# A two-branch transformer block on one core: the order of the first stage rewritten, with 25 identity products ahead of it

## The chip, the core and the metric

The kernel runs on one core of a Trainium2 chip. The core has five engines that run their own instruction streams and meet at semaphores: TensorE (PE in the profile; its weight loads are shown apart as PEld) for matrix products, VectorE (DVE), ScalarE (ACT), GpSimd (POOL), and SyncE (SP), which here issues all DMAs. Products land in PSUM (eight banks); the other operands lie in SBUF; inputs, outputs and larger intermediate results lie in HBM. The metric is the device time of one execution in microseconds, and a kernel's time is the median of its runs.

## What is computed

`x` has 2048 rows of 640 numbers, all in float32. One attention branch with 32 heads of 20 numbers and one MLP branch with shifted columns run on the same layer-normed rows, and both are added to `x`:

```
xn  = layernorm(x)
q, k, v = split(xn @ wqkv)                       # 32 heads of 20
A   = (softmax(q k^T / sqrt(20)) v) @ wo
h   = gelu(layernorm(xn) @ w1)
x1  = xn + shifted(h) @ w2                       # four column groups, rows shifted by +1, -1, +2, -2
B   = x1 + gelu(layernorm(x1) @ w3) @ w4         # w3: 640x1536
out = x + A + B
```

## The kernel before

**Products.** Most products are made in single-pass float32 (fp32r) from operands split in two: a high part (a rounded copy) and a low part (the operand less its high part). A product of two such operands is three: high with high, high with low, low with high. `parts` (L707) lists them for the five 128-row pieces of the contraction, the three of one piece behind each other. `twins` (L711) makes two such sums at once, each on half of the array's rows; it does so in two turns of 15 steps, and between the turns stands a fence (`fence`, L329): a one-element memset on GpSimd (`scratch`) that waits for the first turn's last product and for which the second turn waits. All products, transposes aside, are recorded at L346, and all operations of the other engines at L316.

**Order.** The kernel first lists all operations with their data dependences, a cost and a key (a due time). `schedule` (L389) then plays them through in a small model and emits the program in the order that comes out, engine by engine; each engine keeps that order on the chip. Operations marked `port=True` on VectorE and GpSimd are not planned to overlap, and an operation can be moved to another engine if `alt` says so. For TensorE a string of 7058 letters, `ORDER` (L95), says which kind comes next: `m` a pair of products for the row maxima of the scores, `s` a pair of products for the scores, `p` the products with v, and `d` anything else. Among the `d`s the smallest key that is ready goes first.

**The first stage** (L775 to L911) loads x in 16 tiles of 128 rows (`load_x`, tiles `xb`), the first half of wv in five pieces (`wvr`, of which four borrow the buffers `vst`), and the first 128 columns of wk and wq (`load_w0`). On SP's queue stand two x tiles, wv, two x tiles, wk, wq, and then the other x tiles. `norm_tiles` (L836) takes x tiles in groups: tiles 0 and 1, tiles 2 and 3, then four at a time. Per tile VectorE takes the statistics (two `bn_stats`, one `bn_aggr`). Per group `rsqrt` (L657) makes the reciprocal root: one small VectorE operation, a power on GpSimd (`ry_a`), and three small VectorE operations (`rt_a`, `rt_a`, `lnk`); a fourth makes the bias `lnk[:, 1]`. The tiles are then normalised, the even ones on VectorE and the odd ones on ScalarE, and transposed by TensorE (`tp`); ScalarE rounds the high part of `xT` out of PSUM, and VectorE subtracts the low part. ScalarE rounds and GpSimd subtracts the weights: `split_wv` (L825) for wv, whose subtractions wait for the first group's power, and `load_w0` (L790) for wk and wq (`w0s`), whose subtractions wait for the second group's.

With four tiles transposed, a pair of `twins` makes 512 columns of k and q for the first heads (`ps0`, L880), and two small products (`pk`) put them in the layout of the attention loop. This is done four times. v's first half (`v_half`, L946, tiles `psv`) uses `xT` and wv and can run from the first transposed pair on. The maxima products of the first block then follow among these, and the attention loop starts when that block's 64 pairs of maxima are reduced on VectorE (`mx`).

**Behind it** the attention loop runs over 32 blocks of 32 units, and the `d` products of all other matrices are spread between its products: k, q, v of the other heads, w1 (`w1_phase`, L959, which reads the row factors `r2b` by a DMA for every 512 columns), w2 with the second layernorm (`x1_pair`, `z_pair`), w3 (with `pre3`, gelu and a store), w4 (`w4_phase`, L1147), and last wo (`wo_phase`, L1192).

## Time and profile before

| | |
|---|---|
| median of 3 runs | 1882.86 us (1882.71 to 1885.95) |
| the profiled execution | 1883.12 us |
| its span in the profile | 1881.3 us |
| mean granted TensorE clock | 0.998 |
| DMA moved | 262.00 MB, 139 GB/s over the span |

The profile is one execution. Its page gives each engine's busy time, the span in 40 slices, the chain of work that ended last, and the costliest groups of instructions. A group reads: line, engine, operation, what is written from what, shape, count. A number in square brackets in the timeline is the engine's idle time just before the instruction and what ended it. "Stretches" are windows of the span, in microseconds from its start, with the busy time of each engine. The granted clock is TensorE's, 1.00 being full speed. The ends of matrix products are modelled, so that a busy TensorE is not always one at its peak.

### The profile page before, as it was taken

What the parts mean: (1) busy time and instruction counts of PE and PEld (TensorE: products, weight loads), DVE (VectorE), ACT (ScalarE), POOL (GpSimd) and SP (SyncE); (2) the same over time, 40 slices, a digit from 0 to 9 for tenths busy, and PEclk for the clock granted to TensorE, in tenths of its full rate; (3) what the DMA queues carried; (4) which work ended last, traced back from release to release, by engine and by line L of the source; (5) the groups of instructions that cost most, each with busy time, mean ns of one, the idle gap of its engine ahead of it and who ended that gap; (6) DMA issues with size and microseconds to landing.
All of it is one profiled execution on the core that took longest, in us unless ns stands there. A gap on an engine that the chain in (4) does not pass through costs nothing.

```text
span 1881.3 us, 44229 instructions
## 1 busy us (share of the span) xinstructions
PE 1857.6 (99%) x17185; PEld 1272.1 (68%) x17185; DVE 1568.9 (83%) x2766; ACT 1333.1 (71%) x2456; POOL 383.7 (20%) x586
## 2 busy tenths in 40 slices
PE   6999999999999999999999999999999999999998
PEld 5876666565666657676665757665877777675777
DVE  8979888888889989988788988878887889788724
ACT  4267767877877786777887676778677776768761
POOL 4101111212112112212212311111222222212111
PEclk9999999999999999999999999999999999999999
DMA  4664554646454585655435672434523242343403
GB/s 166 175 169 142 151 120 149 186 147 180 128 156 141 160 230 160 200 155 160 132 126 189 196 223 93 125 101 132 138 72 95 77 115 84 81 132 112 146 13 113
DMA packets 232666, 262.00 MB, mean 139 GB/s; under 512 B 60776, under 2 KB 175928, under 8 KB 230656
## 3 DMA queue, kind: packets, MB, share of 16 engines
q1 hardware_dynamic: 232456, 259.17, 46.7%
q8 instruction: 135, 2.21, 0.5%
q14 instruction: 75, 0.61, 0.1%
HBM read 155.84 MB, written 103.25 MB: 138 GB/s over the span
## 4 chain that ended last, share of the span: by engine, by line
PE 94%; DVE 3%; DMA 2%; ACT 1%; POOL 0%; issue 0%; SPq 0%; DVEq 0%; POOLq 0%; ACTq 0%
PE ps L346 26%; PE pv L346 24%; PE pm L346 14%; PE s L346 14%; PE psv L346 4%; PE pso L346 3%; PE ps_k L346 3%; PE ps_q L346 3%; DVE mx L316 1%; PE psl L346 1%; DMA wd_wo<-ph_wo 0%; DMA wd_w<-ph_w 0%; DMA r2b<-r2d 0%; PE pmt L346 0%; PE c_w L346 0%
## 5 line engine op out<-in xcount | busy, mean ns | idle before, releaser
L316 DVE TENSOR_REDUCE mx<-pm 128x1 f32<-128x512 f32 x2048 | 1281.5, 682 | 195.9 <-PE pm L346 181.4
L316 ACT ACTIVATE p<-s 128x512 f32<-128x512 f32 x2048 | 1080.5, 612 | 282.9 <-PE s L346 237.7
L346 PE MATMUL pv<-p,v 128*32 128x512 f32 x4096 | 494.4, 598 | 0.2 <-DVE mx L316 0.2
L346 PE MATMUL pm<-kpack,zq 60*128 60x512 f32 x2048 | 446.3, 411 | 0.6 <-DVE mx L316 0.5
L346 PE MATMUL s<-zq,kpack 62*128 62x512 f32 x2048 | 443.5, 410 | 1.4 <-ACT p L316 0.8
L346 PE MATMUL ps<-xT,w_w 64*128 64x512 f32 x2040 | 321.5, 394 | 0.0
L346 PEld LDWEIGHTS s<-zq,kpack 62*128 62x128 f32 x2048 | 229.4, 185 | 122.7 <-ACT p L316 39.8
L346 PEld LDWEIGHTS pm<-kpack,zq 60*128 60x128 f32 x2048 | 230.9, 185 | 118.3 <-issue 31.7
L346 PEld LDWEIGHTS pv<-p,v 128*32 128x32 f32 x4096 | 109.2, 109 | 224.4 <-issue 195.2
L346 PEld LDWEIGHTS ps<-xT,w_w 64*128 64x128 f32 x2040 | 211.8, 186 | 34.6 <-issue 2.9
L316 POOL TENSOR_TENSOR ob<-ob,obq 128x512 f32<-128x512 f32 x96 | 123.7, 1289 | 391.5 <-ACT obq L316 292.3
L346 PE MATMUL ps<-xT 64*128 64x320 f32 x1632 | 166.3, 307 | 0.0
L346 PEld LDWEIGHTS ps<-xT 64*128 64x128 f32 x1632 | 145.2, 186 | 10.5 <-issue 1.7
L346 PE MATMUL ps<-xT,gT 64*128 64x320 f32 x1152 | 121.0, 307 | 0.0
L316 ACT COPY obq<-pv 128x512 f32<-128x512 f32 x75 | 44.1, 588 | 106.2 <-PE pv L346 105.9
L346 PEld LDWEIGHTS ps<-xT,gT 64*128 64x128 f32 x1152 | 107.7, 186 | 6.2 <-DVE mx L316 0.8
L334 POOL MEMSET scratch<- 1x1 f32 x134 | 11.9, 89 | 432.6 <-PE ps L346 220.0
L346 PE MATMUL psv<-wv,xT 64*128 64x320 f32 x960 | 92.4, 310 | 0.0
L346 PEld LDWEIGHTS psv<-wv,xT 64*128 64x128 f32 x960 | 82.5, 186 | 6.2 <-POOL scratch L334 1.0
L316 POOL TENSOR_TENSOR ph_w<-pr_w,ph_w 128x320 fp32r<-128x320 f32 (+2 forms) x54 | 40.6, 752 | 210.7 <-ACT ph_w L316 157.5
L346 PE MATMUL ps_q<-xT,w_q 64*128 64x512 f32 x480 | 77.4, 394 | 0.0
L346 PE MATMUL ps_k<-xT,w_k 64*128 64x512 f32 x480 | 75.1, 395 | 0.0
(172 smaller groups left out, 1355.0 us busy)
## 6 DMA issues: line engine op xcount, KB each, us to landing
zq<-qd SPq DMA_DIRECT2D x156, 80.0 KB
kpack<-kd SPq DMA_DIRECT2D x78, 160.0 KB
w_w<-wd_w SPq DMA_DIRECT2D x48, 256.0 KB
gd<-pre SPq DMA_DIRECT2D x8, 1536.0 KB
g<-gd SPq DMA_DIRECT2D x64, 192.0 KB
wd_w<-ph_w SPq DMA_DIRECT2D x34, 320.0 KB
xT<-wd_w SPq DMA_DIRECT2D x34, 320.0 KB
vd<-vst SPq DMA_DIRECT2D x32, 256.0 KB
```

The lines of the kernel that those rows point to most:

```text
L316: getattr(e, m)(val(out), *[val(x) for x in ins], **{k: val(v) for k, v in kw.items()})
L334: o.insts = [nc.gpsimd.memset(scratch.get(), 0.0)]
L346: o.insts = [nc.tensor.matmul(out.get(), lhsT.get(), rhs.get(), **kw) for out, lhsT, rhs, kw in products]
```

## The change

In the first stage:

- SP issues four x tiles, then wv, wk and wq, then the other x tiles.
- `norm_tiles` is cut in two, `norm_rows` (statistics, roots, normalising) and `turn_tiles` (transposes, high and low parts). The rows of tiles 0 to 3 are listed ahead of their transposes, in two groups as before. Statistics of tile 4 are planned behind the second group's bias, and the low parts of tiles 0 and 1 behind the start of the second root.
- The subtractions on GpSimd of all five wv pieces, wk and wq wait for the second group's bias.
- A group `warm` of 25 products of the identity with itself (float32, 128x128) is put on TensorE; it needs only the identity, and its result is not read.
- `phases` lists a sum's products so that all five pieces of one kind (high with high, and so on) stand together. The first k/q products and v take the products with a low weight last.
- VectorE's root operations are planned with `port=True`, and the memsets of `vst` without.

Farther on: `r2b` is read once in four DMAs instead of for each of 20 tiles; the ring of `x1` has 2 buffers instead of 3; the odd shifted tiles (`hs`), `pre3` and `r` get pools of their own, opened before the pool ahead of them is closed; in `w4_phase` the even tiles instead of the odd ones put `gT` in `xT`, and the first product of a tile waits for the buffer of `r`. `ORDER` has 7059 letters: one `d` more and as many `m`, `s` and `p` as before; most of its lines differ, by letters moved a few places, and the last 582 letters are the same.

```diff
+WARM = 25
+WVE = 0
...
-    "dddddddddddddddddd")
+    "ddddddddddddddddddd")
...
+    ps = ps_x.shared([P, 512], F32, "warm", "s")
+    pl.group("full", WARM * 320.0, [(ps[:, :P], ident, ident, dict(start=True, stop=True))] * WARM)
...
-    def rsqrt(pool, v, n, nm, out=None):
+    def rsqrt(pool, v, n, nm, out=None, port=True):
...
+    def phases(lhs, rhs, kts, ab):
+
+        return [(lhs(a, k), rhs(b, k)) for a, b in ab for k in kts]
...
-    load_x(2)
+    load_x(4)
...
-    load_x(2)
-    pl.key += 1
     load_w0(1, "k0")
     load_w0(0, "q0")
...
-            pl("pool", c_pool(320), "tensor_sub", vw0[1][:, 1, i, :], wvr[i], _f(vw0[1][:, 0, i, :]),
-               port=True).deps.append((after, 1))
+            wvs.append(pl("pool", c_pool(320), "tensor_sub", vw0[1][:, 1, i, :], wvr[i], _f(vw0[1][:, 0, i, :]), port=True))
...
-    def norm_tiles(ts):
+    def norm_rows(ts):
...
+        if ts[0] == 2:
+            pl.key -= 2
         for j, t in enumerate(ts):
             stats(lnp, xbs[t], mva[:, t, :], f"a{t}")
+            if t == 4:
+                for o in pl.ops[-3:-1]:
+                    o.deps.append((nbs[-1], 0))
...
         rsqrt(lnp, mva[:, tr, 1], n, g, lnk[:, 0, tr])
+        rvs.append(next(o for o in pl.ops[first:] if o.eng == "dve"))
+        nb = pl("dve", 140.0, "scalar_tensor_tensor", lnk[:, 1, tr], mva[:, tr, 0], -1.0, lnk[:, 0, tr],
+                op0=ALU.mult, op1=ALU.mult, port=True)
+        nbs.append(nb)
         if ts[0] == 0:
-            split_wv(pl.ops[-5])
-        if ts[0] == 2:
-            for o in w0s:
-                o.deps.append((pl.ops[-5], 1))
...
+            split_wv()
+        for o in {0: wvs[:WVE], 2: wvs[WVE:] + w0s}.get(ts[0], ()):
+            o.deps.append((nb, 1))
...
+    def turn_tiles(ts):
...
-            pl("dve", c_dve(m * n * P), "tensor_sub", l, v, _f(h))
+            o = pl("dve", c_dve(m * n * P), "tensor_sub", l, v, _f(h))
+            if ts[0] == 0:
+                o.deps.append((rvs[1], 0))
...
-            norm_tiles(range(4 * tb + g[0], 4 * tb + g[1]))
+        for g in gs:
+            norm_rows(g)
+        for g in gs:
+            turn_tiles(g)
...
-        twins(pss, [parts(lambda p, k: w0[e][:, p, k, :], lambda p, k: xT[:, p, k, sl], range(ND)) for e in (1, 0)], 512)
+        twins(pss, [phases(lambda p, k: w0[e][:, p, k, :], lambda p, k: xT[:, p, k, sl], range(ND),
+                           ((0, 0), (0, 1), (1, 0))) for e in (1, 0)], 512)
...
-        pl("pool", 500.0, "memset", v, 1.0, port=True)
+        pl("pool", 500.0, "memset", v, 1.0)
...
-            twins(pss, [parts(lambda p, k: xT[:, p, k, t * P:(t + 1) * P], lambda p, k: w[:, p, k, :], range(ND))
-                        for t in (t2, t2 + 1)], 320)
+            twins(pss, [phases(lambda p, k: xT[:, p, k, t * P:(t + 1) * P], lambda p, k: w[:, p, k, :], range(ND),
+                               ((0, 0), (1, 0), (0, 1))) for t in (t2, t2 + 1)], 320)
...
+        r2b = wp.tile([P, S], F32, name="r2b")
+        for tb in range(4):
+            dma(r2b[:, tb * 512:(tb + 1) * 512], r2row[:, tb * 512:(tb + 1) * 512].to_broadcast([P, 512]), 262144)
...
-                x1 = sp.tile([P, 2, D], F32, tag="x1", name=f"x1_{q}", bufs=3)
+                x1 = sp.tile([P, 2, D], F32, tag="x1", name=f"x1_{q}", bufs=2)
...
-                    ring.append(sp.tile([P, GB, S // 2], F32, tag="pre3", name=f"pre3_{half}_{f}", bufs=2))
+                    ring.append(rp.tile([P, GB, S // 2], F32, tag="pre3", name=f"pre3_{half}_{f}", bufs=2))
...
-            if t % 2:
+            if t % 2 == 0:
...
-            twins(pss, [parts(lambda p, k: gT[p][k], lambda p, k: w4v(k, n)[:, p, :], range(NF)) for n in range(2)], 320)
+            twins(pss, [parts(lambda p, k: gT[p][k], lambda p, k: w4v(k, n)[:, p, :], range(NF)) for n in range(2)], 320,
+                  room=r)
```

More of the change, by code (lines that the diff above doesn't have):

```diff
@@ L823, in tile_kernel, with split_wv @@
     load_x(XB - 4)
-    def split_wv(after):
+    def split_wv():
         k, pl.key = pl.key, -903.0
@@ L857, in norm_tiles @@
         pl.key += 4
+    def turn_tiles(ts):
+        n = len(ts)
         w = 512 // (P * n)
@@ L1045, in w23_phase @@
         xrp = pl.pool(name="xrp", bufs=2)
-        sp = None
         hs0 = hs_load(0)
         st1.close()
+        rp = None
         for half in range(2):
-            sp = pl.pool(name=f"s3p{half}", bufs=2, side="right")
+            sp = pl.pool(name=f"s3x{half}", bufs=2, side="right")
+            if rp:
+                rp.close()
+            hsp = pl.pool(name=f"s3h{half}", bufs=1, side="right")
             def x1_pair(q, hs):
-                x1 = sp.tile([P, 2, D], F32, tag="x1", name=f"x1_{q}", bufs=3)
+                x1 = sp.tile([P, 2, D], F32, tag="x1", name=f"x1_{q}", bufs=2)
                 mv = sp.tile([P, 2, 2], F32, tag="mv3", name=f"mv3_{q}")
@@ L1099, in w23_phase @@
             z_pair(4 * half + 3, prev)
+            hsp.close()
             sp.close()
@@ L1107, in w23_phase @@
                 gs = [load_g(gp, 0)]
+            rp = pl.pool(name=f"s3r{half}", bufs=2)
             sp = pl.pool(name=f"s3q{half}", bufs=2, side="right")
@@ L1145, in tile_kernel, with w4_phase @@
     W4_ALL = [(k, n) for k in range(NF) for n in range(2)]
-    def w4_phase(gp, gs):
+    def w4_phase(gp, gs, pre):
         fill["part"] = "w4"
+        rp = pl.pool(name="s4r", bufs=2, side="right")
+        pre.close()
         sp = pl.pool(name="s4p", bufs=1, side="right")
@@ L1178, in w4_phase @@
         sp.close()
+        rp.close()
         xtp.close()
```

152 lines of the change are left out of this document (77 added, 75 removed).

## The prediction

> **What bounds the kernel now.** I read the page first, then stretches of the span by engine, then the timeline of the first 33 us, then who waits for whom. From the page:
>
> ```profile
> span 1881.3 us, 44229 instructions
> PE 1857.6 (99%) x17185; PEld 1272.1 (68%) x17185; DVE 1568.9 (83%) x2766; ACT 1333.1 (71%) x2456; POOL 383.7 (20%) x586
> PE 94%; DVE 3%; DMA 2%; ACT 1%; POOL 0%; issue 0%; SPq 0%; DVEq 0%; POOLq 0%; ACTq 0%
> ```
>
> TensorE (PE) is busy for all but 23.7 us and carries 94% of the chain that ended last. To shorten the span one must remove products, make them faster, or fill those 23.7 us. The stretches tell where they lie (length, busy time and instructions of each engine, granted TensorE clock, DMA share, GB/s):
>
> ```profile
> 0.00:11.53 11.53, 0.00 (x1) 0.03 (x1) 6.58 (x15) 4.42 (x7) 10.47 (x35) 1.00 0.85 266
> 11.53:14.73 3.20, 3.17 (x16) 2.54 (x16) 2.40 (x7) 1.44 (x4) 1.18 (x2) 1.00 1.04 395
> 14.73:21.56 6.83, 3.47 (x40) 2.96 (x38) 6.83 (x15) 2.75 (x5) 4.44 (x5) 1.00 0.67 253
> 21.56:28.38 6.82, 6.32 (x28) 4.69 (x30) 6.82 (x25) 0.95 (x3) 1.01 (x1) 0.50 0.29 97
> 28.38:32.91 4.53, 4.19 (x35) 2.86 (x34) 2.54 (x9) 1.47 (x2) 1.23 (x2) 1.00 0.01 4
> 32.91:50.00 17.09, 16.73 (x124) 12.85 (x125) 16.14 (x40) 12.95 (x24) 1.09 (x2) 1.00 0.32 115
> 50.00:1850.00 1800.00, 1797.28 (x16642) 1222.19 (x16639) 1510.54 (x2621) 1307.32 (x2413) 360.46 (x521) 1.00 0.47 138
> 1877.00:1881.30 4.30, 0.00 (x0) 0.00 (x0) 0.76 (x2) 0.00 (x0) 0.00 (x0) 1.00 0.44 167
> ```
>
> From 50 to 1850 us TensorE lacks 2.72 us in 1800. The last 4.30 us are the output leaving, which the change does not touch. So the first 33 us hold the rest: 15.8 us idle, and a stretch of 6.82 us at half clock (0.50), in which 28 products ran where the full clock could have run about twice as many. What happens there (start, length, engine, operation, what the idle time before waited for):
>
> ```profile
> 1.02 0.29 POOL masks.py:199 TENSOR_SCALAR_AFFINE_SELECT ident<-ident 128x128 f32<-128x128 f32 x1
> 3.55 0.89 DVE L316 BATCH_NORM_STATS2 bn_a<-xb 128x6 f32<-128x320 f32 x2 [3.55 <-DMA xb<-in_A_x_dram]
> 5.01 0.89 DVE L316 BATCH_NORM_STATS2 bn_a<-xb 128x6 f32<-128x320 f32 x2 [0.33 <-DMA xb<-in_A_x_dram]
> 6.42 0.72 POOL L316 TENSOR_TENSOR ry_a<-rv_a,mhalf 128x2 f32<-128x2 f32 x1
> 7.11 3.30 POOL L316 TENSOR_TENSOR wv<-vst,wv 128x320 fp32r<-128x320 f32 x4
> 7.17 0.81 DVE L316 SCALAR_TENSOR_TENSOR rt_a<-ry_a 128x2 f32<-128x2 f32 x1 [0.83 <-POOL ry_a L316]
> 9.65 0.78 DVE L316 SCALAR_TENSOR_TENSOR lnk<-mva,lnk 128x2 f32<-128x2 f32 x1
> 10.46 0.92 ACT L316 ACTIVATE xb<-xb,lnk 128x640 f32<-128x640 f32 x1 [1.87 <-DVE lnk L316]
> 11.39 0.56 DVE L316 TENSOR_SCALAR xb<-xb,mva,lnk 128x640 f32<-128x640 f32 x1
> 11.53 2.37 PE L316 MATMUL tp<-ident,xb 128*128 128x128 f32 x10 [11.53 <-ACT xb L316]
> 13.29 1.35 ACT L316 CAST xT<-tp 128x512 fp32r<-128x512 f32 x3 [1.91 <-PE tp L316]
> 13.93 2.92 PE L346 MATMUL psv<-wv,xT 64*128 64x320 f32 x30
> 15.12 0.15 DVE L316 SCALAR_TENSOR_TENSOR rt_a<-ry_a 128x2 f32<-128x2 f32 x1
> 15.34 1.56 POOL L316 TENSOR_TENSOR w_k<-wr_k,w_k 128x640 fp32r<-128x640 f32 x1 [0.90 <-ACT w_k L316]
> 15.52 1.41 DVE L316 SCALAR_TENSOR_TENSOR rt_a<-rt_a,rv_a 128x2 f32<-128x2 f32 x1
> 16.87 1.52 POOL L316 TENSOR_TENSOR w_q<-wr_q,w_q 128x640 fp32r<-128x640 f32 x1
> 17.25 1.16 DVE L316 SCALAR_TENSOR_TENSOR lnk<-rt_a,ry_a 128x2 f32<-128x2 f32 x1
> 18.98 1.16 DVE L316 TENSOR_SCALAR xb<-xb,mva,lnk 128x640 f32<-128x640 f32 x1
> 20.19 1.32 PE L316 MATMUL tp<-ident,xb 128*128 128x128 f32 x10 [3.34 <-DVE xb L316]
> 22.82 0.79 PE L346 MATMUL ps<-xT,w_k 64*128 64x512 f32 x1 [0.50 <-DVE xT L316]
> 29.21 0.50 PE L346 MATMUL ps<-xT,w_q 64*128 64x512 f32 x1 [0.34 <-POOL scratch L334]
> 32.84 2.40 PE L316 MATMUL tp<-ident,xb 128*128 128x128 f32 x20
> ```
>
> Three things are to be seen. **One:** VectorE's four small operations after each root take 0.15 us when alone (15.12), but 0.8 us at 7.17 to 9.65, where GpSimd subtracts wv, and 1.41 and 1.16 us beside w_k and w_q. So tiles 0 and 1 are normalised late, and tiles 2 and 3 later still: their root starts only when x tiles 2 and 3, loaded behind wv, are through VectorE at 13. **Two:** TensorE idles 11.53 us, then 3.34 us, and then only after ten more transposes (20.19) come the first k/q products, at 21.53; the next stand until 22.82. **Three:** half clock follows, so that the first turn of those products takes from 22.82 to about 28.9, and the second turn, at full clock, from 29.21 to 32.91: 3.70 us for 15 steps, 0.24 us each.
>
> The Trainium skill, page "SBUF — State Buffer", section "SBUF: two separate sides", says that VectorE and GpSimd share one port pair as an exclusive lock, taken by a VectorE operation with two SBUF inputs when GpSimd reads SBUF. The rows agree (0.81 against 0.15); by it, GpSimd's later subtractions could still block x2's normalising once, for one subtraction of 0.83 us.
>
> **The change part by part.** The sum is made against this execution (1881.3 us of span, 1883.12 us as a run; the median of the three runs is 1882.86).
>
> *Loads.* The same loads are issued on SP; two x tiles go ahead of five wv pieces. x0 and x1 land as now (3.55, 5.01). For the rest the stream in the first 20 us in half-microsecond slices:
>
> ```profile
> GB/s 0 0 0 97 323 318 256 320 356 374 397 341 279 225 246 330 297 265 296 331 347 352 365 374 399 394 405 399 399 384 405 389 399 394 399 384 374 292 174 46
> ```
>
> Summed, 1.31 MB (four tiles) is reached at 5.8 us; x1's last byte was reached about 1 us before its statistics began, so x3 is usable near 6.8. Piece by piece wv is usable from 7.3 to 9.7. wk, wq and everything behind see the same bytes ahead of them, so nothing is paid there; wv has cover, since its low half is wanted much later.
>
> *First root.* GpSimd's power still ends at 7.14. Four operations at 0.16 us, with x3's statistics (0.89 as at 5.01, and 0.2 to aggregate) slipping in between: 7.17 + 0.6 + 1.1 = 8.9, against 10.43 now. Bounds: 7.8 and 10.4.
>
> *Second root.* Its first operation follows at 9.0; power 0.70 and its start 0.25: 10.0; four operations and some of x0's normalising (0.56) between: 11.3, against 18.88. Bounds 10.6 and 12.5. x3's normalising on ScalarE (0.92) gives 12.2, ten transposes at full clock (2.40 us for 20) 13.4, and two of ScalarE's three casts (1.35) 14.3. The k/q products start at 14.3 instead of 21.53.
>
> *GpSimd's subtractions behind the second root.* Queued behind that wait are five of wv (0.83 each, 4.2 us), w_k 1.56 and w_q 1.52: from 11.5 to 15.7, 17.3 and 18.8. TensorE waits for them only for products with a low weight, which the new order by phases puts last: ten of a turn's 15 steps (2.4 us, 14.3 to 16.7) need none. So the turn's last five wait until 19.0 and end at 20.2. The fence between the turns (0.34 us of idle before 29.21; I take 0.6 with its way there and back) gives 20.8, and the second turn's 3.70 us **24.5 instead of 32.91, 8.4 us won**. The 2.3 us wait at 16.7 and the hole before 14.3 have cover: 30 psv products, which are in the count of 32.91 also (2.92 us), and of whose successors some fit. I take 1.0 us for these, bounds 0 and 2.2 (another 30 at full clock).
>
> *The 25 identity products.* They add TensorE work where it idles. The nearest row, four identity products of the last stage, recorded as two passes each:
>
> ```profile
> 1850.52 1.16 PE L346 MATMUL pb<-ident,rx 128*128 128x128 f32 x8
> ```
>
> That is 0.29 us a product at full clock. Ten transposes took 2.37 us at 11.53, before the clock came, and 1.32 at 20.19, so a cold product is 0.52. From 1.5 us (ident is ready at 1.31) 25 products end at 8.8 if none is cold, at 10.2 with 3.2 us of slow clock as from 11.53 to 14.73, and at 11.8 with 6.8 us, the length of the one half-clock stretch. The first transposes could begin at 9.9. So nothing is paid: even 1.9 us of delay moves the first ten steps to end at 18.6, before the low weights at 19.0. Without that cover it would be those 1.9 us. What they buy is in the sum already: a full clock for transposes and products.
>
> On that clock the row is the half rate from 21.56 to 28.38 after 3.34 us without a product. The Trainium skill, page "TensorE: Matmul & The Clock Gate", Part 1, says the gate opens after a busy window of about 3.4 us and closes after an idle one. By it the pause between warm products and k/q products would have to stay under 3.4 us; in the trace 3.34 us were enough to lose the clock, so the page's bound is no safe one here. That is the first rival.
>
> *The rest.* x1's ring of 2 for 3, another pool for pre3 and r, the other gT first, roots planned as port users, memsets not: no instruction is added. The most there is to win from 50 us on is the 2.72 us. x1's shorter ring is covered, because a pair's transposes end before the pair after next is written:
>
> ```profile
> 733.86 1.31 PE L316 MATMUL tz<-ident,x 128*128 128x128 f32 x10
> 752.98 0.99 DVE L316 SCALAR_TENSOR_TENSOR x<-xr,lnk,ps 128x320 f32<-128x320 f32 x2
> 672.75 0.69 DVE L316 TENSOR_TENSOR pre<-ps,r2b 128x512 f32<-128x512 f32 x1 [2.21 <-DMA r2b<-r2d]
> ```
>
> There are 18 us between them; without that cover a product group would wait. Reading r2b once (4 DMAs for 20) takes away the last row's stall on VectorE, of which TensorE felt part: 0.5 us, bounds 0 and 2.2. The written order has one letter more (the warm group) and equal counts of the other three kinds: nothing for switching.
>
> Sum: 8.4 + 1.0 + 0.5 = 9.9 us; 1883.12 - 9.9 = 1873.2, and 0.3 less as a median: **1873**. With the bounds of each term 1869.5 to 1877.
>
> **The rivals.** *Half clock again* (A): after the warm products TensorE has 10 transposes and few products until 14.3, and one more window of 6.82 us falls to 0.50. Price half of it, 3.4 us: 1876.4. For it: the row of 21.56. Against: the holes are shorter than 3.34 us if psv fills them.
>
> *GpSimd is the bound* (B): the subtractions come later than 11.5 or queue behind a fence, and the five wv ones stand ahead of w_k. One such round is 4.2 us: 1877.2. For it: the path already ends in w_q at 18.8. Against: rows of equal length now, and phases.
>
> *VectorE is the bound until block 0's maxima are done* (C):
>
> ```profile
> 75.00:95.40 20.40, 20.40 (x257) 19.22 (x255) 20.23 (x34) 3.05 (x9) 1.54 (x6) 1.00 0.92 215
> ```
>
> It has 0.17 us to spare there, so the attention loop starts when VectorE is through. If all it gains is its stretched operations (2.5 us of the first four, 1.3 + 1.0 + 0.6 of 15.52, 17.25 and 18.98), 5.4 us are won: 1877.7. Against: of the 4.53 us from 28.38 it idled 2.0 as well, and TensorE has psv to run meanwhile.
>
> *More than that* (D): the second root ends at its early bound (0.7 us more), the holes fill wholly (2.2) and the later 2.7 us vanish too: 14.0 us won, 1869.
>
> *Slower* (E): TensorE takes its instructions in a written order, made anew in most of its lines. Between 50 and 1850 us it waits almost nowhere, while VectorE is at 84% and ScalarE at 73%, so an order that asks for a maximum or a score a little early stalls everything behind it. The longest sort of wait now, from 50 to 1850 (total, times, longest):
>
> ```profile
> PE s L346 <- ACT p L316: 0.8, 1, 0.8
> ```
>
> At 0.5 us a wait, 26 of them among 2048 such pairs cost 13 us, 3 more than is won: 1886. It decides from about 20 on. Against: the letters' counts and the last 582 of them are unchanged.
>
> **How the numbers follow.** Likeliest 0.53; A 0.12, B 0.12, C 0.10, D 0.06, E 0.07. This kernel's measurement can tell about 0.2% (3.8 us) from nothing. Below 1879.1: the likeliest, D, and nearly all of A, B and C: 0.87; within: 0.07, from C and E's mild end; slower 0.06. The range 1867.5 to 1880 holds the likeliest, D and A to C.
>
> **What would show it.** Right: a first k/q product near 14 and its twin ended near 24.5; the small operations of both roots at 0.15 to 0.2 us; no 0.50 in the clock after the warm products; TensorE's busy time from then on unchanged. Wrong: a half-clock window between 10 and 30 (A); TensorE waiting for w_q beyond 19 (B); waits for maxima between 60 and 95 (C); PE idle time from 50 to 1850 above 12 us (E).

## The result, and the profile after

| | median us | runs | ratio to the kernel before, same chip, 95% interval |
|---|---|---|---|
| predicted | 1873.0 (1867.5 to 1880) | | 0.995 |
| changed kernel | 1884.01 (1880.57 to 1890.47) | 14 | 1.0007 (1.0000 to 1.0014) |
| changed kernel, a second set | 1881.25 (1878.25 to 1886.58) | 12 | 1.0000 (0.9988 to 1.0012) |

The change made no difference that can be told. The kernel before had medians of 1883.14 and 1881.75 us beside these two sets. The forecast of 10 us less was wrong.

The profiled execution of the changed kernel took 1885.77 us, 1883.9 of them its span. Lines of the same code have moved by two (L316 is now L318, L346 is L348). From its page the span, the engines and the chain:

```profile
span 1883.9 us, 44336 instructions
...
PE 1863.1 (99%) x17235; PEld 1279.9 (68%) x17235; DVE 1555.5 (83%) x2761; ACT 1338.2 (71%) x2458; POOL 397.2 (21%) x589
...
PE 92%; DVE 3%; DMA 3%; issue 1%; SPq 0%; POOL 0%; ACT 0%; DVEq 0%; POOLq 0%; ACTq 0%
```

Then two stretches of it (length, busy time and instructions of each engine, clock, DMA share, GB/s):

```profile
0.00:50.00 50.00, 42.75 (x318) 34.97 (x320) 42.95 (x118) 25.50 (x45) 22.59 (x48) 0.97 0.53 185
50.00:1850.00 1800.00, 1791.33 (x16582) 1220.17 (x16582) 1494.93 (x2605) 1310.33 (x2410) 369.45 (x522) 1.00 0.46 135
```

From 50 to 1850 us TensorE now idles 8.67 us where it idled 2.72, and it ran 60 products fewer in that stretch. What was won ahead of it was given back inside it. The place is found by comparing the start of the n-th `pv` product in two traces (there are 4096 in each). Where the kernel before is at 250, 600, 1000, 1250, 1550 and 1840 us, another kernel leads (minus) or lags by so many us:

```
                          250    600   1000   1250   1550   1840
changed kernel           -3.9    1.1    0.9    2.5    3.6    2.6
the same, second trace   -4.2   -0.9   -2.2   -4.2   -3.1   -4.2
e1_first_only            -4.9   -4.1   -3.8   -5.0   -4.9   -5.0
e2_rest_only             -0.8    1.8    2.7    2.4    2.9    1.9
e3_sync                  -6.8   -4.1   -3.0   -3.7   -2.1   -3.1
e4_nowarm                -4.1   -1.6   -1.0   -1.8    0.0   -0.9
f2_oldorder              -5.3   24.3   33.0   31.8   34.9   36.6
f1_first_sync            -8.7   -5.4   -5.5   -6.7   -6.6   -6.9
f1_again                 -8.0   -9.1  -10.1   -9.5   -9.4   -9.8
f3_first_sync_nowarm     -7.7   -7.7   -6.3   -7.5   -5.9   -6.4
f4_first_sync_pools      -8.0   -9.5   -9.0  -10.2   -7.0   -5.0
f5_first_sync_r2b        -8.9   21.6   29.2   27.9   28.0   27.8
g1_hlh                   -8.2   -3.8   -3.1   -5.2   -4.1   -5.0
g2_three                 -7.4   -5.9   -5.9   -7.5   -7.7   -8.7
g4_four                  -7.2   -5.8   -4.9   -7.1   -7.2   -8.1
```

The first row says two things. The first stage won 4 us, not 9.4; and more than that was lost between 320 us and the end. (In the second trace the lead falls from 4.2 to 0.9 us and comes back, so the size of the second loss changes from one execution to the next.) The rest of this section shows both in the trace.

**The first stage.** Its timeline (start, length, engine, operation, what the idle time before waited for):

```profile
7.26 0.49 DVE L318 BATCH_NORM_STATS2 bn_a<-xb 128x6 f32<-128x320 f32 x1 [1.48 <-DMA xb<-in_A_x_dram]
...
8.73 0.14 DVE L318 SCALAR_TENSOR_TENSOR rt_a<-ry_a 128x2 f32<-128x2 f32 x1
...
9.80 1.07 POOL L318 TENSOR_TENSOR ry_a<-rv_a,mhalf 128x2 f32<-128x2 f32 x1 [1.18 <-DVE lnk L318]
...
10.84 3.32 POOL L318 TENSOR_TENSOR wv<-vst,wv 128x320 fp32r<-128x320 f32 x4
...
10.90 0.83 DVE L318 SCALAR_TENSOR_TENSOR rt_a<-ry_a 128x2 f32<-128x2 f32 x1 [0.59 <-POOL ry_a L318]
...
13.40 0.78 DVE L318 SCALAR_TENSOR_TENSOR lnk<-mva,lnk 128x2 f32<-128x2 f32 x1
...
14.10 1.23 DVE L318 TENSOR_SCALAR xb<-xb,mva,lnk 128x640 f32<-128x640 f32 x1
...
15.39 2.40 PE L318 MATMUL tp<-ident,xb 128*128 128x128 f32 x10 [2.95 <-DVE xb L318]
...
16.09 1.54 POOL L318 TENSOR_TENSOR w_k<-wr_k,w_k 128x640 fp32r<-128x640 f32 x1 [1.12 <-ACT w_k L318]
...
19.23 1.57 POOL L318 TENSOR_TENSOR w_q<-wr_q,w_q 128x640 fp32r<-128x640 f32 x1 [1.59 <-ACT w_q L318]
...
20.05 0.39 PE L348 MATMUL ps<-xT,w_k 64*128 64x512 f32 x1
...
24.50 0.50 PE L348 MATMUL ps<-xT,w_q 64*128 64x512 f32 x1 [0.70 <-POOL scratch L336]
```

The first root's operations are short now (0.14 at 8.73). The second root's are not: 0.83 us at 10.90 to 0.78 at 13.40. GpSimd's subtraction of wv starts at 10.84, right after the second power and ahead of the bias it was said to wait for, which ends at 14.18. The dependence in the change orders the planner's list; no wait on the chip comes out of it. So the old collision has moved from the first root to the second, x2 is normalised at 14.10, and TensorE idles 2.95 us before the transposes at 15.39, which then run at half clock (2.40 us for ten; the record of the clock has 0.50 from 15.05 to 18.47).

**The stretch behind it.** The waits that took the lead stand at four places. The stretches around them:

```profile
320.00:345.00 25.00, 22.93 (x200) 13.45 (x198) 20.09 (x36) 15.48 (x26) 4.46 (x5) 0.93 0.65 155
...
655.00:690.00 35.00, 32.30 (x246) 19.98 (x244) 29.04 (x50) 25.12 (x45) 4.22 (x9) 0.95 0.94 246
...
1095.00:1120.00 25.00, 23.20 (x164) 10.60 (x158) 17.25 (x31) 20.43 (x42) 2.13 (x2) 0.93 0.86 226
...
1295.00:1312.00 17.00, 16.80 (x97) 5.71 (x95) 13.74 (x24) 15.96 (x24) 6.78 (x7) 0.90 0.92 308
```

The first of them in the timeline:

```profile
334.89 0.33 DVE L318 CAST ph_w<-pr_w 128x320 fp32r<-128x320 f32 x1 [2.72 <-DMA wd_w<-ph_w]
335.13 0.68 DVE L318 COPY ob<-pv 128x512 f32<-128x512 f32 x1
...
335.87 1.39 PE L348 MATMUL pm<-kpack,zq 60*128 60x512 f32 x4 [1.96 <-DVE ob L318]
```

And two entries of the chain of waits (start, length):

```profile
325.41 9.36 DMA wd_w<-ph_w
...
660.26 9.07 DMA qd<-hl_q
```

VectorE takes its list in order. At 334.89 it rounds the next weight piece into a buffer (`ph`, a ring of one) from which a store issued at 325.41 is still being read; it stands for 2.72 us, the copy `ob` and the maxima stand behind it, and TensorE waits 1.96 us. At 669 it is the store of `hl_q`. At 1112 it is probably that of wo, issued at 1103.75; the profile names no releaser there. Each wait is followed by a window of half clock, and so is the stretch at 1301. Two of the four, with the window ahead:

```profile
332.49:335.90 3.41, 1.45 (x30) 0.81 (x27) 1.01 (x3) 2.46 (x6) 1.43 (x2) 1.00 0.80 265
335.90:339.32 3.42, 3.42 (x20) 1.34 (x24) 3.42 (x6) 0.00 (x0) 1.49 (x2) 0.50 0.77 265
...
1301.88:1305.29 3.41, 3.21 (x14) 1.10 (x16) 3.15 (x6) 3.40 (x7) 1.27 (x1) 1.00 1.04 412
1305.29:1308.70 3.41, 3.41 (x18) 1.03 (x14) 1.55 (x4) 2.98 (x8) 0.00 (x0) 0.50 0.82 294
```

In the windows at 1301 and 1305 PE is shown as busy, yet it ran 14 and 18 products in them, where its mean over the stretch from 50 us is 31. Where ends are modelled, the count of products shows a wait that the busy time hides. This fourth place is not peculiar to the new order: f3_first_sync_nowarm and f4_first_sync_pools below, which have the old one, fall to half clock there too (at 1294.78 and 1292.81).

### The profile page after: what moved, and what is told of

It reads as the page before. It is cut to its first block, busy times and chain, and to the rows that moved or that the text cites. A ratio compares the mean times of both kernels' runs of the same rounds, so it can differ in the third digit from the quotient of the medians.

```text
span 1883.9 us, 44336 instructions
## 1 busy us (share of the span) xinstructions
PE 1863.1 (99%) x17235; PEld 1279.9 (68%) x17235; DVE 1555.5 (83%) x2761; ACT 1338.2 (71%) x2458; POOL 397.2 (21%) x589
## 3 DMA queue, kind: packets, MB, share of 16 engines
q8 instruction: 135, 2.21, 0.5%
## 4 chain that ended last, share of the span: by engine, by line
PE 92%; DVE 3%; DMA 3%; issue 1%; SPq 0%; POOL 0%; ACT 0%; DVEq 0%; POOLq 0%; ACTq 0%
PE ps L348 26%; PE pv L348 24%; PE s L348 14%; PE pm L348 14%; PE psv L348 4%; PE pso L348 3%; PE ps_k L348 3%; PE ps_q L348 3%; DVE mx L318 2%; PE psl L348 1%; DMA wd_w<-ph_w 1%; DMA kpack<-kd 1%; DMA qd<-hl_q 0%; DMA xb<-in_A_x_dram 0%; SPq L318 0%
## 5 line engine op out<-in xcount | busy, mean ns | idle before, releaser
L318 DVE TENSOR_REDUCE mx<-pm 128x1 f32<-128x512 f32 x2048 | 1282.4, 683 | 211.6 <-PE pm L348 195.6
L318 ACT ACTIVATE p<-s 128x512 f32<-128x512 f32 x2048 | 1081.1, 611 | 283.0 <-PE s L348 238.0
L348 PE MATMUL pv<-p,v 128*32 128x512 f32 x4096 | 495.7, 600 | 0.1
L348 PE MATMUL pm<-kpack,zq 60*128 60x512 f32 x2048 | 444.6, 411 | 5.9 <-DVE ob L318 4.1
L348 PE MATMUL s<-zq,kpack 62*128 62x512 f32 x2048 | 448.6, 412 | 1.3 <-ACT p L318 0.5
L348 PE MATMUL ps<-xT,w_w 64*128 64x512 f32 x2040 | 323.6, 395 | 0.4 <-DVE mx L318 0.3
L348 PEld LDWEIGHTS s<-zq,kpack 62*128 62x128 f32 x2048 | 230.8, 186 | 128.6 <-DVE mx L318 36.3
L348 PEld LDWEIGHTS pm<-kpack,zq 60*128 60x128 f32 x2048 | 230.4, 185 | 117.1 <-DVE mx L318 28.7
L348 PEld LDWEIGHTS pv<-p,v 128*32 128x32 f32 x4096 | 110.2, 109 | 225.3 <-issue 196.8
L348 PEld LDWEIGHTS ps<-xT,w_w 64*128 64x128 f32 x2040 | 213.2, 187 | 32.7 <-issue 2.5
L318 POOL TENSOR_TENSOR ob<-ob,obq 128x512 f32<-128x512 f32 x96 | 124.9, 1302 | 400.5 <-ACT obq L318 310.9
L348 PE MATMUL ps<-xT 64*128 64x320 f32 x1632 | 167.5, 307 | 0.0
L348 PEld LDWEIGHTS ps<-xT 64*128 64x128 f32 x1632 | 149.5, 186 | 9.8 <-issue 3.4
L348 PE MATMUL ps<-xT,gT 64*128 64x320 f32 x1152 | 119.4, 307 | 0.0
L318 ACT COPY obq<-pv 128x512 f32<-128x512 f32 x74 | 43.6, 590 | 103.0 <-PE pv L348 100.8
L348 PEld LDWEIGHTS ps<-xT,gT 64*128 64x128 f32 x1152 | 104.7, 186 | 6.1 <-issue 0.8
L348 PE MATMUL psv<-wv,xT 64*128 64x320 f32 x960 | 91.9, 310 | 0.3 <-ACT xT L318 0.3
L348 PEld LDWEIGHTS psv<-wv,xT 64*128 64x128 f32 x960 | 81.2, 186 | 6.8 <-POOL scratch L336 1.4
L348 PE MATMUL ps_q<-xT,w_q 64*128 64x512 f32 x480 | 80.8, 399 | 0.0
L348 PE MATMUL ps_k<-xT,w_k 64*128 64x512 f32 x480 | 75.5, 394 | 0.0
L318 POOL TENSOR_TENSOR ph_w<-pr_w,ph_w 128x320 fp32r<-128x320 f32 (+2 forms) x47 | 35.9, 765 | 157.5 <-ACT ph_w L318 117.1
```

The lines of the kernel that those rows point to most:

```text
L318: getattr(e, m)(val(out), *[val(x) for x in ins], **{k: val(v) for k, v in kw.items()})
L348: o.insts = [nc.tensor.matmul(out.get(), lhsT.get(), rhs.get(), **kw) for out, lhsT, rhs, kw in products]
```

## The experiments

Two theories stood at the start. *Theory 1*: the first stage wins 4 us and not 9.4 since nothing on the chip holds the subtractions back. *Theory 2*: the later edits and the written order lose the rest. The rival to the second was that any early lead is given back further on. Fourteen sets were run, two of them repeats of a kernel:

| kernel | median us | runs | ratio, 95% interval |
|---|---|---|---|
| e1_first_only | 1880.33 | 9 | 0.9978 (0.9966 to 0.9990) |
| e2_rest_only | 1885.26 | 12 | 1.0004 (0.9995 to 1.0013) |
| e3_sync | 1878.27 | 8 | 0.9969 (0.9958 to 0.9979) |
| e4_nowarm | 1879.56 | 11 | 0.9981 (0.9971 to 0.9991) |
| f1_first_sync | 1874.29 | 5 | 0.9956 (0.9944 to 0.9968) |
| g1_hlh | 1881.48 | 12 | 0.9994 (0.9982 to 1.0005) |
| g2_three | 1877.75 | 11 | 0.9974 (0.9965 to 0.9983) |
| f2_oldorder | 1919.69 | 4 | 1.0197 (1.0184 to 1.0210) |
| after_again | 1881.25 | 12 | 1.0000 (0.9988 to 1.0012) |
| g4_four | 1877.66 | 12 | 0.9975 (0.9963 to 0.9987) |
| f3_first_sync_nowarm | 1875.45 | 9 | 0.9969 (0.9958 to 0.9979) |
| f1_again | 1875.58 | 7 | 0.9968 (0.9953 to 0.9982) |
| f4_first_sync_pools | 1880.17 | 12 | 0.9987 (0.9978 to 0.9995) |
| f5_first_sync_r2b | 1911.35 | 4 | 1.0154 (1.0141 to 1.0168) |

(after_again is the changed kernel itself, f1_again is f1_first_sync itself.)

### The two halves of the change apart

e1_first_only is the kernel before with the edits in the first stage and `"d"` put ahead of its written order; e2_rest_only has only the others (r2b, pools, gT, new written order).

```diff
 # e1_first_only, against before: hunks of the first stage, and
+ORDER = "d" + (ORDER of before)
 # e2_rest_only, against before: the hunks from w1_phase on, and
+ORDER = (ORDER of after)[1:]
```

> The first-stage edits alone (identity products, four x tiles ahead of wv, GpSimd's subtractions placed later), with the written order of the rest, the r2b, x1, hs, pre3, r and gT edits as before. Theory 1 (the first stage wins about 4.3 us on the chip and not 9.4, because nothing on the chip holds the subtractions back): the k and q products again start near 20 us and the lag against the kernel before is about -4 us at 100 us. Theory 2 (the rest of the loss is laid down in the later written order and pools): the lead of 4 us then stays to the end and the time is 1878 to 1880. Rival (any early lead is given back because VectorE then meets stores that have not landed, whatever the later order): 1883 or more, with new PE waits of about 2 us behind VectorE and half-clock windows after 300 us.

> The later edits alone: the changed written order after its first entry, r2b loaded once, the pools for x1, hs, pre3 and r, and gT; first stage as before. If the later written order by itself makes VectorE meet unlanded stores, the time is 1886 to 1889 (the 6.9 us given back between 320 and 1310 us, less what depends on the early lead), with new half-clock windows after 300 us. If the loss needs the early lead, the time is within 1 us of before, 1883.

Theory 2 holds in the main. The first stage alone leads by 4.9 us at 250 and still by 5.0 at the end (its median, 1880.33, is just above what was expected); in the trace of the other edits alone there is a lag of 1.9 there, though the interval of its ratio does not tell its time from that of the kernel before. TensorE's idle time between 50 and 1850 us, first of e1_first_only, then of e2_rest_only:

```profile
50.00:1850.00 1800.00, 1797.25 (x16651) 1221.42 (x16649) 1507.06 (x2619) 1307.31 (x2410) 360.89 (x524) 1.00 0.47 137
```

```profile
50.00:1850.00 1800.00, 1792.64 (x16606) 1223.35 (x16606) 1497.58 (x2608) 1312.24 (x2413) 372.03 (x525) 1.00 0.46 135
```

That is 2.75 us with the early lead and 7.36 without it, so most of the waits belong to the later edits, not to an early start. Not all: at 320 to 345 us the early lead seems to cost something under the old order too, 1.9 us in e1_first_only (of which 1.1 are back at 600) and 3.3 in f1_first_sync below. The time of e2_rest_only, 1885.26, is a little under the 1886 to 1889 expected. Its trace is 2.7 us ahead at 100, because the half clock of the first stage happened to last 3.41 us in it (20.50 to 23.91) and not 6.83, and from there to the end it loses 4.6.

### A true wait for the subtractions

e3_sync is the changed kernel in which the seven subtractions wait on the chip for the second root's bias.

```diff
             o.deps.append((nb, 1))
+            o.hold = nb
...
+            if o.hold is not None:
+                self.tc.add_manual_dep(o.insts[0].ins, o.hold.insts[-1].ins.name, SYNC)
```

> The changed kernel with one true wait on the chip: GpSimd's weight subtractions wait for the second root's bias. If the port collision of these subtractions with the second root's four short operations is what kept the k and q products at 20 us, those four take 0.14 instead of 0.8 us each, the transposes of the later tiles start about 2.5 us sooner (near 12.9) with no half-clock window at 15 to 18.5, the first product of k and q comes at 15 to 17.5 us and the time falls by 2 to 4 us against the changed kernel, to 1880 to 1882. Rival (the weights or w_q set the first product, whatever the root does): first product still at 19.5 to 20.5 or later, time 1884 to 1885.

Its timeline, at the places shown above for the changed kernel:

```profile
9.28 1.07 POOL L319 TENSOR_TENSOR ry_a<-rv_a,mhalf 128x2 f32<-128x2 f32 x1 [1.18 <-DVE lnk L319]
...
10.38 0.16 DVE L319 SCALAR_TENSOR_TENSOR rt_a<-ry_a 128x2 f32<-128x2 f32 x1 [0.59 <-POOL ry_a L319]
...
10.97 0.16 DVE L319 SCALAR_TENSOR_TENSOR lnk<-mva,lnk 128x2 f32<-128x2 f32 x1
...
11.28 3.62 POOL L319 TENSOR_TENSOR wv<-vst,wv 128x320 fp32r<-128x320 f32 x4 [0.92 <-ACT wv L319]
...
11.86 0.77 PE L319 MATMUL tp<-ident,xb 128*128 128x128 f32 x5
...
15.52 0.39 PE L351 MATMUL ps<-xT,w_k 64*128 64x512 f32 x1
```

Theory 1 holds, in every step of the first stage: the subtractions start at 11.28 instead of 10.84, the four operations take 0.16 us each, the transposes stand at 11.86 instead of 15.39 and at full clock, and the first k/q product comes at 15.52 instead of 20.05. At 250 us the lead is 6.8 us instead of 3.9. The bias now ends at 11.13 (10.97 + 0.16), the prediction's 11.3, and the second turn at 24.94, the prediction's 24.5 (28.23 in the changed kernel). The median, 1878.27, fell further than the 1880 to 1882 expected.

f1_first_sync puts the same wait into e1_first_only, and f1_again is that kernel once more.

> The first-stage edits alone, as in e1_first_only, with the true wait of e3_sync added. If the two parts add up, the wait's 3.5 us of lead (e3_sync against the changed kernel at 100 us) come on top of the 5.0 us that e1_first_only kept to its end: a lead of 7.5 to 8.5 us at 100 us, kept to the end, time 1876 to 1877. Rival (a lead above some 5 us is always given back further on, since VectorE then meets its stores unlanded in the old order too): 1879 to 1881, with new PE waits behind VectorE of 2 us or more.

> f1_first_sync (first-stage edits and the true wait, everything later as before) once more, beside the two that add one later edit each. If its 8 us are no accident of one execution: 1873 to 1876, ratio to the kernel before 0.994 to 0.997.

The parts add up: a lead of 8.0 to 8.7 us at 250 and, where no half-clock window fell (f1_again's profile), 9.8 at the end. In the trace of f1_first_sync 3.3 us of it went at one place, much as the rival had it, though behind a load: VectorE stood 2.53 us for `sm`, TensorE behind it for 1.95 us, and half clock fell at 332.71. That left 6.9 at the end.

```profile
331.13 0.25 DVE L319 RECIPROCAL rc<-sm 128x16 f32<-128x16 f32 x1 [2.53 <-DMA sm<-od]
```

The stretches of f1_again show the lead being kept:

```profile
0.00:50.00 50.00, 44.60 (x348) 36.77 (x350) 42.60 (x120) 25.41 (x45) 22.89 (x49) 1.00 0.53 187
50.00:1850.00 1800.00, 1798.04 (x16679) 1222.98 (x16677) 1507.04 (x2621) 1307.21 (x2410) 359.18 (x525) 1.00 0.47 138
```

This version beats both kernels: 1874.29 and 1875.58 us, ratios of 0.9956 and 0.9968.

### The 25 identity products

e4_nowarm takes them out of the changed kernel, f3_first_sync_nowarm out of f1_first_sync.

```diff
-    ps = ps_x.shared([P, 512], F32, "warm", "s")
-    pl.group("full", WARM * 320.0, [(ps[:, :P], ident, ident, dict(start=True, stop=True))] * WARM)
```

> The changed kernel without the 25 identity products. If they only hold the clock up, the first 25 us run at half clock longer: the transposes of the first tiles take twice as long and the first turn starts at or after 20 us; time +1 to +3 us against the changed kernel (1885 to 1887). Rival (the clock in the first 20 us costs nothing since VectorE sets the pace): within 0.5 us of the changed kernel.

> f1_first_sync without the 25 identity products: their worth by itself, on the version that keeps its lead. If they hold the clock up for the first transposes and first-stage products (full from 4.8 us with them), the time is 1.5 to 4 us above f1_first_sync: 1876 to 1878. Rival (VectorE, ScalarE and GpSimd set the pace till the first k and q products, and the clock is up by then anyway): within 0.7 us of it, 1874 to 1875.

In the changed kernel they win nothing: leads of 4.1 us at 250 without them, 3.9 and 4.2 with them, since the idle 2.95 us before 15.39 loses the clock that they brought. On the version with the wait they are worth 0.3 to 1.0 us (7.7 against 8.0 and 8.7), less than the 1.5 us expected; the medians do not tell the two apart (f3's lies 1.2 us above f1_first_sync's and 0.1 below f1_again's). e4_nowarm's median lies 1.7 and 4.5 us below the two sets of the changed kernel, where 1 to 3 us above was expected. The interval of its ratio is apart from the first set's and overlaps the second's, and the mean clock of its 11 runs is 0.998 to 1.000, that of the changed kernel's 26 runs 0.994 to 0.998 (the half clock at 15.05 is 0.001 of the difference). So the products may even cost time there. Why is not shown: the lead at the end of e4_nowarm's trace, 0.9 us, lies between those of the changed kernel's two traces, which differ by 6.8 us with the same program.

### Which of the later edits

f2_oldorder is the changed kernel with the written order of before. f4_first_sync_pools adds to f1_first_sync the pool edits alone (x1's ring of 2, the pools of `hs`, `pre3` and `r`, gT's other half), f5_first_sync_r2b only the single load of `r2b`.

```diff
 # f5_first_sync_r2b, against f1_first_sync
+        r2b = wp.tile([P, S], F32, name="r2b")
+        for tb in range(4):
+            dma(r2b[:, tb * 512:(tb + 1) * 512], r2row[:, tb * 512:(tb + 1) * 512].to_broadcast([P, 512]), 262144)
...
-                    r2b = wp.tile([P, 512], F32, tag="r2b", name=f"r2b{c}_{tb}", bufs=1)
-                    dma(r2b, r2row[:, tb * 512:(tb + 1) * 512].to_broadcast([P, 512]), 262144)
```

> The changed kernel with the written order of the kernel before (one entry for the identity products put ahead of it); r2b loaded once and the pool edits stay. If the written order itself makes the waits, this keeps the first stage's 4 to 5 us to the end: 1878 to 1880. Rival (taking the r2b reload away lets VectorE reach the multiplications and then the roundings sooner, under either order, and it then meets the unlanded stores): a wait of 2 to 4 us at 660 to 670 us for the store of hl_q here too, time 1882 to 1885.

> f1_first_sync with the pool edits (x1, hs, pre3, r, and gT's half) alone, old written order, r2b reloaded as before. If the pool edits are what gives the lead back, a wait behind VectorE or the stores appears after 300 us and the time is 3 us or more above f1_first_sync, 1877 to 1881. Rival (they touch nothing that PE waits for; the loss is in the order and r2b): within 1 us of f1_first_sync, 1873 to 1876.

> f1_first_sync with r2b loaded once alone, old written order, pools as before. If taking the r2b reload away is what lets the gelu, the roundings and their exponentials collide with PE's list under the old order (the 36 us that f2_oldorder lost between 330 and 710 us), this loses them too: 1900 to 1912. Rival (the loss of f2_oldorder came from the pool edits under the old order): within 2 us of f1_first_sync, 1873 to 1877.

f2_oldorder came out outside both expectations, 37 us slower than before, so it could not say which edit is at fault; the other two can. The single load of `r2b`, which takes 16 DMAs away, costs 36 us under the old order (1911.35 against 1875.58 on the same chip). In its list of waits between 320 and 720 us TensorE stands for ScalarE's exponentials (total us, times, longest):

```profile
PE s L351 <- ACT p L319: 6.6, 6, 1.5
PE s L351 <- DVE mx L319: 1.7, 2, 1.4
PE pm L351 <- ACT p L319: 1.6, 2, 1.1
```

f1_again has in that stretch 399.75 us of busy TensorE and 3378 products, f5_first_sync_r2b 386.04 and 3018, at a clock of 0.97. Six stretches of half clock, 27.3 us together, stand in its trace, and none in f1_again's. Without the reload the planner puts VectorE's multiplications `pre`, and with them the gelu, at other places, and TensorE's list, which was written for the former places, meets the exponentials late. In f1_again's trace the second `pre` of each pair stands 6 to 12 row-maxima reductions behind the first, in f5_first_sync_r2b's right behind it, and the ten gelus of w1 come 8 to 13 exponentials sooner there (the first behind the 274th instead of the 284th).

The pool edits cost 4.6 us under the old order (1880.17 against 1875.58; the lead goes from 10.2 us at 1250 to 5.0 at the end). The intervals of the two ratios, 0.9978 to 0.9995 and 0.9953 to 0.9982, just overlap; the traces agree with the medians. Of these 5.2 us 2.8 go between 1290 and 1320, where half clock falls; which of the pool edits does it was not tried. So neither of these edits is free. The new written order makes up for most of it, not for all: with it, the trace of all later edits together ends 1.9 us behind the kernel before (e2_rest_only). Which entries of the order would have to change was not tried.

### Moving the roundings that wait

after_again is a second trace of the changed kernel, to see whether the places recur.

> The changed kernel once more, unaltered, for a second trace of it. If the PE waits at 334, 668, 1112 and 1305 us and the half-clock windows behind them belong to its written order, all four waits stand at the same places again with 0.5 to 4 us each; which of them is followed by a half-clock window may differ, since that depends on where the windows of 3.41 us fall. Time 1881 to 1887. Rival (they were an accident of the one profiled execution): other places, or none.

The waits at 333 and 666 stand there again (1.03 and 1.89 us of idle TensorE), and at 1298 half clock falls again; the one at 1112 stays under half a microsecond, and another of 1.28 us stands at 678.85. Of the half-clock windows behind them only that at 1298 is left. Two windows at 666, and that one:

```profile
663.62:667.03 3.41, 2.72 (x25) 1.02 (x17) 1.08 (x2) 2.17 (x3) 0.00 (x0) 1.00 1.04 388
667.03:670.45 3.42, 2.21 (x18) 1.81 (x20) 3.30 (x6) 1.85 (x4) 2.43 (x2) 1.00 1.04 350
...
1298.50:1301.91 3.41, 3.41 (x18) 1.03 (x14) 1.46 (x3) 2.90 (x7) 0.00 (x0) 0.50 0.92 348
```

Here the wait at 666 straddles two windows, and they keep 2.7 and 2.2 us of work. So the same program ended 4.2 us ahead of the kernel before in one trace and 2.6 behind in the other.

Then the roundings at which VectorE waited in e3_sync were put later in its list, after planning. g1_hlh moves `hlh_4_2` (the one at 661.5 us), g2_three also `ph_w2_1_1` (329) and `ph_wo_4_0` (1106), g4_four also `hlh_4_3` on ScalarE. `behind` puts an operation, with all that needs it, behind the next n operations of its engine.

```diff
 # g4_four, against e3_sync
+MOVES = (("ph_w2_1_1", 4), ("hlh_4_2", 7), ("hlh_4_3", 5, "act"), ("ph_wo_4_0", 4))
...
     def emit(self):
-        for o in self.schedule():
+        order = self.schedule()
+        for m in MOVES:
+            order = self.behind(order, *m)
+        for o in order:
```

> e3_sync with one more edit: after the planner is done, the rounding of hlh_4_2 (the one that waits 4.15 us for the store of hl_q near 661.5 us) is put seven VectorE instructions later, with what needs it. If this one place in VectorE's list is what costs the new order its lead there, PE's wait of 3.8 us at 662 and the half-clock window after it go, the lead at 700 to 1100 us is 3 to 5 us larger than in e3_sync (-3.0 us against the kernel before), and the time is 1874 to 1876. Rival (VectorE or the transfers only shift the wait): another wait of about the same size within 20 us, time within 1 us of e3_sync, 1878.

> As g1_hlh, and in the same way the rounding of ph_w2_1_1 (1.5 us of wait at 329) four instructions later and that of ph_wo_4_0 (2.0 us at 1106) four later. If every wait of VectorE for an unlanded store is paid by PE, another 1 us at each of the two places: 1872 to 1875. Rival (PE has enough queued work at these two): no difference from g1_hlh beyond 1 us.

> As g2_three, and in the same way the second rounding of that pair, hlh_4_3, which ScalarE holds and at which it waited 2.6 us for the store of hl_q in g2_three (3.2 us in g1_hlh) with the exponentials p behind it, is put five ScalarE instructions later. If the wait had only gone from VectorE's list to ScalarE's, PE's wait of 2.0 us at 662 and its half-clock window now go, and the time is 1871 to 1875 (2 to 4 us below g2_three). Rival (p and the maxima are late there for another reason, such as the table loads beside the gelu): PE's wait at 662 stays at 1.5 us or more and the time within 1 us of g2_three, 1877 to 1879.

None of the three was faster than e3_sync. g1_hlh (1881.48) came out above both forecasts, and the interval of its ratio lies above e3_sync's; why it was slower is not shown. At 329 and 1106 the waits did go in g2_three, which is 3.7 us below g1_hlh, so its rival did not hold; its profile keeps a lead of 8.7 us, but that execution was the fastest of its 11, and its median (ratio 0.9974) can't be told from e3_sync's (0.9969). g4_four's time, 1877.66, is its rival's. At 662 the wait only went elsewhere. First e3_sync, where VectorE waits; then g1_hlh, where ScalarE does; then g4_four:

```profile
665.69 0.43 DVE L319 CAST hlh<-pre 128x512 fp32r<-128x512 f32 x1 [4.15 <-DMA qd<-hl_q]
```

```profile
666.17 0.62 ACT L320 CAST hlh<-pre 128x512 fp32r<-128x512 f32 x1 [3.23 <-DMA qd<-hl_q]
...
667.34 0.50 PE L353 MATMUL pm<-kpack,zq 60*128 60x512 f32 x2 [2.47 <-ACT p L320]
```

```profile
667.52 0.73 PE L353 MATMUL ps_q<-xT,w_q 64*128 64x512 f32 x4 [1.32 <-POOL scratch L341]
...
673.57 0.40 ACT L320 CAST ph_w<-pr_w 128x256 fp32r<-128x256 f32 x1 [3.51 <-DMA wd_w<-ph_w]
...
674.53 0.50 PE L353 MATMUL s<-zq,kpack 62*128 62x512 f32 x1 [2.56 <-ACT p L320]
```

With both roundings of the pair moved, the next rounding waits for the next store, 3.51 us. Late transfers are what stays: from 650 to 680 us the DMA engines are taken to 0.84 to 0.97 in all these kernels. f1_again is at 0.94 too, and its TensorE still idles only 0.25 us there. In its order the roundings of this pair come at 665.78, 16.3 us after the store they need (issued at 649.43), in the changed kernel 9.2 us after it (660.26 to 669.42), 2.73 of them spent waiting. What comes ahead of them in f1_again is the second multiplication, which waits there for the reload of `r2b` and is planned 8 row-maxima reductions behind the first:

```profile
662.69 0.69 DVE L319 TENSOR_TENSOR pre<-ps,r2b 128x512 f32<-128x512 f32 x1 [1.24 <-DMA r2b<-r2d]
...
665.78 0.75 DVE L319 CAST hlh<-pre 128x512 fp32r<-128x512 f32 x2
```

All 16 traces fit a reload that keeps the roundings away from the store. In the six with the reload of `r2b` no `hlh` rounding is seen waiting for the store of `hl_q`; in nine of the ten without it one is, for 1.0 to 4.4 us at the longest. The tenth is g4_four, where both roundings were moved.

## Why the prediction was wrong, step by step

- **Loads, first root.** Near: the statistics of x2 began at 7.26, and the first bias ended at 9.79 (9.64 + 0.15) against 8.9 predicted, inside the bounds of 7.8 to 10.4. The power did not end at 7.14, but at 8.61: in VectorE's list the statistics of x2, which waited 1.48 us for their load, stood ahead of the root.
- **Second root: failed.** The step "GpSimd's subtractions behind the second root's bias", from 11.5 on, took a dependence of the planner for a wait on the chip. They started at 10.84, stretched the root's four operations to 0.8 us each, and the k/q products began at 20.05, not 14.3. With the wait made true the bias ended at 11.13 (11.3 predicted), the products began at 15.5, and the lead at 250 us was 2.6 to 3.8 us larger. Of the 9.4 us of the sum's first two terms the changed kernel so had 3.9 to 4.2. With the wait it has 6.8, and with the old order besides 8.7 and 8.0 (f1_first_sync, f1_again, where the second turn ended at 24.60 and 25.36 against 24.5 predicted). So with the wait that they took for granted these terms were nearly right.
- **The clock (A).** Half clock did come back, from 15.05 to 18.47 us, behind the 2.95 us of idle TensorE that the collision made. In e3_sync and f1_first_sync there is none ahead of 300 us.
- **The identity products.** Right that they cost nothing in the first stage: they ended at 8.84, before the first transposes at 10.37. The clock that they buy was overrated.
- **B and C.** In f1_again TensorE waited 0.48 us for w_q at 19.23, which is B's sign at a small size, and from 30 to 95 us never for maxima. So GpSimd's queue held the stage up by no more than that there, and VectorE not at all.
- **"Nothing for switching", "another pool ... no instruction is added", r2b worth +0.5: failed.** This step and the second root share the loss. The second root took 5.2 to 5.5 of the 9.4 us; the later edits then took about 4 to 5.5, by the ratios of the changed kernel (1.0007, 1.0000) and of e1_first_only (0.9978). The old written order fitted the old program: the single load of `r2b` by itself costs 36 us under that order, the pools 4.6, and with the new order the trace of all of them still loses 4.6 us between 100 us and the end. The stall on `r2b` whose end was counted as a gain of 0.5 us had a use: it spaced the gelu out between the exponentials and kept the roundings far enough behind the stores that they wait for.
- **E, given 0.07, is the rival that came nearest**, but by another mechanism than it named: not some 26 half-microsecond waits for maxima, but a few of 2 us behind a store, on each of which a window of half clock may follow. PE's idle time from 50 us on, 8.67 us, stayed below the 12 that were to show E. The half clock behind those waits was in no rival.

The Trainium skill, page "SBUF — State Buffer", section "SBUF: two separate sides", and the traces agree once more on the lock between VectorE and GpSimd: the same four operations take 0.16 us or 0.8, with the subtractions behind or beside them.

## What to carry to other kernels

A dependence in a planner is a wait on the chip only if a semaphore comes out of it: look in the trace whether the held instruction starts after its releaser. An order written for one program is part of that program, so an edit that adds no instruction, or takes a stall away, has to be priced together with the order; run the halves of a change apart before judging it. Where an in-order engine needs a buffer that a store still reads, moving one instruction can hand the wait to the next one (at 662 us it did, at 329 and 1106 it did not), unless the time between the store's issue and the buffer's reuse grows.

## What the hardware showed that was not expected

A wait of about 2 us can cost the clock for 3.41 us. In every trace with several starts of half clock these lie a whole number of 3.413 us apart, so the windows can be laid out from them. In the changed kernel windows with 1.45 us of work in 3.41 (332.49) were followed by half clock, and so were 1.34 us (667.00) and 1.73 us (1110.73):

```profile
667.00:670.41 3.41, 1.34 (x9) 0.77 (x9) 0.99 (x3) 0.81 (x2) 0.48 (x1) 1.00 1.07 392
1110.73:1114.14 3.41, 1.73 (x12) 0.43 (x12) 1.30 (x3) 2.79 (x6) 0.86 (x1) 1.00 0.90 296
```

Windows with 2.21 and 2.72 us of work in the second trace were not. In f5_first_sync_r2b one of 2.38 us was, and one of 1.97 us was not:

```profile
513.23:516.64 3.41, 2.38 (x11) 0.70 (x11) 2.52 (x5) 3.40 (x8) 0.00 (x0) 1.00 0.65 153
427.90:431.31 3.41, 1.97 (x13) 0.53 (x12) 2.59 (x5) 3.38 (x7) 0.74 (x1) 1.00 0.73 210
```

So it depends on where a wait falls against the windows, and the busy time shown, with its modelled ends, gives no sharp threshold. The clock goes with the time: in the second set of the changed kernel the three runs with a mean clock of 0.994 or 0.995 took 1885.03 to 1886.58 us, the four with 0.997 or 0.998 1878.25 to 1880.61. The spread of runs by itself says little of these waits: the 14 runs of the changed kernel span 9.9 us, but 18 runs of the kernel before, beside f1_again, span 12.2. The Trainium skill, page "TensorE: Matmul & The Clock Gate", Part 1, says that the window of 3413 ns runs freely and that the clock falls after an idle one; the length agrees with the 3.41 us here, but a window did not have to be idle: 1.73 us of work in it were not enough.
